# Placing the k-transpose-v tiles of a linear attention in other passes of its projection loop

## The chip, the cores and the metric

One NeuronCore of a Trainium2 chip runs the whole program as one launch. The metric is the device time of the launch in microseconds, taken as the median of several runs. PE stands for TensorE (its weight loads are shown as PEld), DVE for VectorE, ACT for ScalarE, POOL for GpSimd and SP for SyncE, whose queue issues nearly all DMAs.

## What is computed

The input x has 2048 rows of 640 elements, in bf16. The reference, cut to what matters:

```python
x = A_x
h  = x + A_ref(layernorm(x), wqkv, w_phi, wo)
h2 = h + (gelu(ln(h) @ w_gate) * (ln(h) @ w_up)) @ w_down

# A_ref: 32 heads of 20
q, k, v = split(x @ wqkv)
phi_q = concat(softmax(q @ w_phi), softmax(-(q @ w_phi)))     # per head, 40 features
phi_k = concat(softmax(k @ w_phi), softmax(-(k @ w_phi)))
kv = phi_k^T v          # per head, summed over all 2048 rows
z  = sum(phi_k)         # over all rows
o  = (phi_q kv) / (phi_q z + 1e-6)
return o @ wo
```

No row's attention output can be had before `kv` and `z` have been summed over all rows.

## The kernel before

Rows are worked in 16 tiles t of 128. `w_phi` is folded into the k and q weights on the chip (`fold`, L221), so `Wk2` and `Wq2` give the features' logits directly.

**The projection loop (L462 to L511) makes one pass per tile t.** `k_tile(t)` (L312) runs 10 matmuls into a PSUM tile `pk`, and ACT makes of it exp(x) and exp(-x), the tile `E` (two activations, L317). `v_mm(t+4)` runs 10 matmuls for the v of a later tile and `v_ev` (ACT, L304) copies it to `vS`. `ln_ap(t+6)` (ACT, L143) normalizes a later tile, and SP sends it through a transposing DMA into `LN1T` (L159), from which `v_mm` and `k_tile` read. `k_norm(t)` (L320) sums `E` per head on DVE (`sk`, L324), inverts the sums (`rs`, L328) and multiplies them into v, on POOL and DVE (`vt`, L332). `E` and `vt` have 8 buffers each.

**`kv_tile(i)` (L344) adds tile i to the sum.** It issues 40 small matmuls (128 rows by 32 columns of `E` against 42 or 63 columns of `vt`), each with its own weight load, thus 80 PE instructions, into one PSUM bank `kvp` that lives from pass 3 to the end of the loop. PE executes its instructions in the order in which the code issues them, so `KVG` (L56) says behind which pass's `k_tile` the sums of which tiles run: tiles 0 to 2 in pass 6, 3 to 5 in pass 9, 6 to 8 in pass 12, 9 to 11 in pass 15, and the last four after the loop (L513). Within a pass the order on PE is `k_tile(t)`, a fold of a part of `Wq2` (passes 10 to 14), the `kv_tile`s, then in pass 15 the q groups, then `v_mm(t+4)` (passes 1 to 11).

**The q groups.** `q_mm(j)` (L364) computes the q logits of group j of `QG` for 512 rows: two blocks of 5 matmuls of 512 columns for groups 0 to 2, one block for group 3. `q_exp(j)` (L376) lets ACT make the two exponentials `Eq`. `QT` (L53) puts groups 0 to 3 in pass 15. PSUM is shared by `pk`, `pv`, the fold and `pq` through 3 rotating tiles of two banks (`psG`, L465).

**After the loop** `kv_mask()` (L355, DVE) masks the sum into the matrix `KV`, the PSUM pools are closed and a pool of 4 tiles is opened (L520). PE goes on with the first block of q group 4 (L755), whose PSUM tile lies where group 3's was, with the first attention tile (`attn_a(0)`, matmuls at L562 on `KV` and `Eq`), and then with the remaining q groups, the attention tiles, and the feed-forward part (`gate_up` L685, `down` L702).

SP's queue in passes 7 to 13 carries, in this order, the transposes of the normalized tiles, those of the q weights (`load_T(WqT, ...)`, L194, in passes 7 to 10 by `LQ`), three small copies of `kmask` (L505), and the loads of `Wo` and `Wg` (L510, L511). The fold in pass 14 reads the last part of `WqT`.

Of the kernel before, what the change touches and what calls it, by code (L numbers as in the profile page):

```python
# [17 lines left out]
def kernel(  # L18
# [19 lines left out]
    NT = S // P  # L38
# [14 lines left out]
    QT = (15, 15, 15, 15)  # L53
    T3 = 3

    KVG = {6: (0, 1, 2), 9: (3, 4, 5), 12: (6, 7, 8), 15: (9, 10, 11)}  # L56
    VC = Dh + 1
    KC = Dh + 2

# [131 lines left out]
    def load_T(WT, i, *ds):  # L191

        for d in ds:
            nc.sync.dma_start_transpose(WT[:, :, d * P:(d + 1) * P], A_wqkv[d * P:(d + 1) * P, i * D:(i + 1) * D])  # L194
# [26 lines left out]
    def fold(WT, W2, quarters, ds=range(NC)):  # L221


        n, w = (2, QF) if quarters else (1, HD)
        runs = []
        for c in range(NC):
            lo, hi = H0[c] * Dh, (H0[c] + NH[c]) * Dh
            for r in range(2 * n):
                a, b = max(lo, r * w), min(hi, (r + 1) * w)
                if a < b:  # L230
                    runs.append((r // n, r, c, a, b))
        runs.sort()
        for d in ds:
            wa = gtile("wa")
            wr = wa.rearrange("p u (q x) -> p (u q) x", q=n)
            for i, (u, r, c, a, b) in enumerate(runs):
                nc.tensor.matmul(wr[:, r, a - r * w:b - r * w], lhsT=WT[:, c, d * P:(d + 1) * P],
                                 rhs=BD[:, c].rearrange("p a b -> p (a b)")[:, a - H0[c] * Dh:b - H0[c] * Dh],
                                 start=(i == 0 or runs[i - 1][0] != u),
                                 stop=(i + 1 == len(runs) or runs[i + 1][0] != u), skip_group_check=True)  # L240
            dst, src = W2[:, d, :].rearrange("p (u f) -> p u f", u=2), wr[:, :, 0:w]
            if quarters:
                dst = W2[:, d, :].rearrange("p (c r f) -> p r c f", c=NC, r=4)
                src = src.rearrange("p r (c f) -> p r c f", c=NC)
            if d in (QA if quarters else KA):
                nc.scalar.copy(dst, src)
            else:
                nc.vector.tensor_copy(dst, src)
# [15 lines left out]
    def ln_st(*tiles, act=True, between=None, log=False):  # L264
        for t, v in zip(tiles, ln_stats(p1, [x_sb[t // 4][:, t % 4, :] for t in tiles], "1", act, between, log)):
            lnp[t] = v

    def ln_ap(t, on_act=False, on_pe=False):
        ln = (ln_act if on_act else ln_dve)(p1, "1", *lnp[t])
        if on_pe:  # L270
            lnp[t] = ln
        else:
            transpose_to(LN1T[t // 4][:, :, t % 4 * P:(t % 4 + 1) * P], ln, False)
# [15 lines left out]
    def v_mm(t, us=(0, 1)):  # L289
        if 0 in us:  # L290
            pv[t] = gtile("pv")
        proj(pv[t], t, Wv, us)
# [10 lines left out]
    def v_ev(t):  # L303
        nc.scalar.activation(vS[t % 8][:, :, 0:Dh].rearrange("p (u h) f -> p u h f", u=2),  # L304
                             pv[t][:, :, 0:HD].rearrange("p u (h f) -> p u h f", f=Dh), ACTF.Copy,
                             scale=lnp[t][2] if t in CT else 1.0)
# [5 lines left out]
    def k_tile(t):  # L312
        pk = gtile("pk")
        proj(pk, t, Wk2, rows=t == 0)
        Ek[t] = ev.tile([P, 2, D], BF16, name="E", bufs=8)
        for s in range(2):
            nc.scalar.activation(Ek[t][:, s, :].rearrange("p (u f) -> p u f", u=2), pk[:, :, 0:HD],  # L317
                                 ACTF.Exp, scale=((lnp[t][2], nrstd[t]) if t in CT else (1.0, -1.0))[s])

    def k_norm(t):  # L320


        sk = small(p1, [P, 2 * H], "sk")
        nc.vector.reduce_sum(sk, Ek[t].rearrange("p s (h f) -> p (s h) f", f=Dh), axis=AX.X)  # L324
        if t - 1 in todo:
            todo.pop(t - 1)()
        rs = small(p1, [P, 2 * H], "rs")
        nc.vector.reciprocal(rs, sk)  # L328
        Vt[t] = vt = ev.tile([P, 2, H, VC], BF16, name="vt", bufs=8)

        def mult(s, eng):
            eng.tensor_tensor(vt[:, s], vS[t % 8], rs[:, s * H:(s + 1) * H, None].to_broadcast([P, H, VC]), ALU.mult)  # L332

        mult(1, nc.gpsimd)
        if t in VP:
            mult(0, nc.gpsimd)
        elif t == NT - 1:
            mult(0, nc.vector)
        else:
            todo[t] = lambda: mult(0, nc.vector)  # L340
# [3 lines left out]
    def kv_tile(t):  # L344

        for s in range(2):
            for c in range(NC):
                i, h, n = SLOT[c]
                for r in range(4):
                    f0, h0 = r * QF + c * 32, r * QH + h  # L350
                    nc.tensor.matmul(kvp[QUAD[r], s * SL + i:s * SL + i + n, :],
                                     lhsT=Ek[t][:, s, f0:f0 + 32], rhs=Vt[t][:, s, h0:h0 + n, :],
                                     start=(s == c == t == 0), stop=(t == NT - 1), skip_group_check=True)
# [10 lines left out]
    def q_mm(j, part=(0, 1)):  # L364

        if 0 in part:
            pqs[j] = gtile("pq")
        for i, bc in enumerate(QG[j]):
            if i not in part:
                continue  # L370
            b, c = divmod(bc, NC)
            for kc in range(NC):
                nc.tensor.matmul(pqs[j][:, i, :], lhsT=Wq2[:, kc, c * P:(c + 1) * P], rhs=LN1T[b][:, kc, :],  # L373
                                 start=(kc == 0), stop=(kc == NC - 1))

    def q_exp(j, signs=(0, 1)):  # L376
        for s in signs:
            nc.scalar.activation(Eq[j][:, :, s, :], pqs[j][:, 0:len(QG[j])], ACTF.Exp, scale=(1.0, -1.0)[s])  # L378
# [83 lines left out]
    for t in range(NT):  # L462
        if t == T3:
            ps_cm.close()
            psG = ps_cm.enter_context(tc.tile_pool(name="psG", bufs=3, space=PSUM, reuse_waits="tile"))  # L465
            psK = ps_cm.enter_context(tc.tile_pool(name="psK", bufs=1, space=PSUM, reuse_waits="tile"))
            kvp = psK.tile([P, 2 * SL, VC], F32, name="kvp")
        k_tile(t)
        if t == 0:
            ln_ap(6)  # L470
        if t in FQ:
            fold(WqT, Wq2, True, [i for i, f in enumerate(FQ) if f == t])
        for i in KVG.get(t, ()):
            kv_tile(i)
        for j in range(len(QT)):
            if t == QT[j]:
                q_mm(j)
                q_exp(j)
        if 0 < t < NT - 4:
            v_mm(t + 4)  # L480
        if t > 0 and t + 6 < NT:
            ln_ap(t + 6, on_act=True)
        if 0 < t < NT - 4:
            v_ev(t + 4)
        if t % 2 == 0 and t + 8 < NT:
            ln_st(t + 8, t + 9)
        k_norm(t)
        load_T(WqT, 0, *[i for i, f in enumerate(LQ) if f == t])
        if t == 10:
            transpose_to(LN1T[0][:, :, P:2 * P], ln_a(1), False)  # L490
        if t == 12:
            ln_ap(0, on_act=True)
        if t == 7:
            nc.gpsimd.memset(kmask[QUAD[0]], 1.0)
            for k, lo, n, base in ((3, 0, 2, 0), (2, 6, 3, 12)):
                m = kmask[QUAD[0], lo:lo + 6].rearrange("p (k n) -> p k n", k=k)
                nc.gpsimd.affine_select(out=m, in_=m, pattern=[[4, k], [-Dh, n]],
                                        compare_op=ALU.is_ge, fill=0.0, base=base, channel_multiplier=1)
                nc.gpsimd.affine_select(out=m, in_=m, pattern=[[-4, k], [Dh, n]],
                                        compare_op=ALU.is_ge, fill=0.0, base=Dh - 1 - base, channel_multiplier=-1)  # L500
        if t == 8:
            nc.gpsimd.memset(KV, 0.0)
        if t == 9:
            for r in (1, 2, 3):
                nc.sync.dma_start(kmask[QUAD[r]], kmask[QUAD[0]])  # L505
        if t == 11:
            nc.gpsimd.tensor_copy(KV[:, 0, :, KC - 1], kmask)
            nc.gpsimd.tensor_copy(KV[:, 1, :, 0], kmask)
        if t == 13:
            nc.sync.dma_start(Wo, wo_v)  # L510
            nc.sync.dma_start(Wg, wg_v)  # L511
    q = len(QT)
    for t in range(12, NT):  # L513
        kv_tile(t)
    kv_mask()
    ev_cm.__exit__(None, None, None)
# [341 lines left out]
```

## Time and profile before

| | |
|---|---|
| median of 3 runs | 279.61 us (279.37 to 279.69) |
| the profiled execution: its own time | 280.84 us |
| its span, first to last instruction | 278.9 us |
| PE busy / DVE / ACT / POOL | 97% / 62% / 51% / 34% of the span |
| PE matmuls, weight loads | 2979, 2995 |
| mean granted PE clock | 0.994 |
| instruction-fetch packets, queue q8 | 23, 0.38 MB |

The span leaves out 1.94 us of the execution's own time. In the timeline a row gives the start, the length, the engine, the line, the operation, its output and inputs, the count, and in brackets the idle time before it with what ended it. Matmul ends are modelled, so neighbouring rows of PE overlap a little; for PE the distance between two starts is the safer measure. A run of ten 320-column matmuls is followed by the next one 1.36 us later, a run of ten 512-column ones 2.16 us later.

### The profile page before, as it was taken

How to read it: one execution, taken by the hardware profiler on the slowest of the kernel's cores; microseconds unless marked ns; L12 is line 12 of the kernel's file. 1: busy time of each engine (PE TensorE's matmuls, PEld its weight loads, DVE VectorE, ACT ScalarE, POOL GpSimd, SP SyncE). 2: the span in 40 equal slices, each digit the busy share in tenths (PEclk: the TensorE clock that was granted, in tenths of full speed). 3: DMA queues.
4: the chain of work that ended last, by engine and by line, in shares of the span. 5: the costliest groups of instructions: out<-in, count | busy, mean ns of one | idle time of the engine just before them, and what ended most of it. 6: DMA issues, size and time to landing. Idle time of an engine off the chain costs nothing.

```text
span 278.9 us, 7232 instructions
## 1 busy us (share of the span) xinstructions
PE 270.4 (97%) x2979; PEld 172.5 (62%) x2995; DVE 173.6 (62%) x332; ACT 141.2 (51%) x241; POOL 95.8 (34%) x219
## 2 busy tenths in 40 slices
PE   8999899999699999999999999999999999999996
PEld 4777677764345688778864555575455567444574
DVE  4879999986368586676457874235986432233332
ACT  5789888887379866446533445402445420222200
POOL 4248999674001125645402372202155300000000
PEclk9999999999889999999999999999999999999999
DMA  6963616587049112224211222110213311000011
GB/s 185 205 232 67 72 34 113 54 181 290 5 129 382 58 27 44 53 51 95 49 49 47 27 47 58 38 48 26 49 27 71 46 47 49 24 0 0 2 47 47
DMA packets 42400, 21.46 MB, mean 77 GB/s; under 512 B 35200, under 2 KB 40576, under 8 KB 42368
## 3 DMA queue, kind: packets, MB, share of 16 engines
q1 hardware_dynamic: 41712, 20.98, 31.0%
q8 instruction: 23, 0.38, 0.6%
q10 hardware_dynamic: 656, 0.03, 0.2%
q14 instruction: 9, 0.07, 0.1%
HBM read 10.18 MB, written 2.62 MB: 46 GB/s over the span
## 4 chain that ended last, share of the span: by engine, by line
PE 72%; issue 1%; ACT 0%; DVE 0%
PE gu L694 37%; PE pd L713 19%; PE po L634 8%; PE pq L373 6%; PE ab L562 2%; PE tp L156 0%; ACT Eq L378 0%; DVE y L716 0%
## 5 line engine op out<-in xcount | busy, mean ns | idle before, releaser
L700 DVE TENSOR_TENSOR GT<-gu,g 128x512 bf16<-128x512 f32 (+1 forms) x60 | 34.4, 580 | 47.3 <-PE gu L694 38.5
L697 ACT ACTIVATE g<-gu 128x512 bf16<-128x512 f32 (+1 forms) x60 | 30.7, 512 | 63.7 <-PE gu L694 63.5
L694 PE MATMUL gu<-LN2T,Wg 128*128 128x512 bf16 (+1 forms) x289 | 61.2, 335 | 0.6
L694 PE MATMUL gu<-LN2T,Wu 128*128 128x512 bf16 (+1 forms) x300 | 61.7, 336 | 0.0
L713 PE MATMUL pd<-Wd,GT 128*128 128x320 bf16 (+2 forms) x396 | 53.5, 295 | 0.0
L713 PEld LDWEIGHTS <-GT 128*128 128x128 bf16 x396 | 37.9, 98 | 14.6 <-DVE GT L700 0.2
L694 PEld LDWEIGHTS <-Wu 128*128 128x128 bf16 x300 | 29.4, 98 | 22.6
L694 PEld LDWEIGHTS <-Wg 128*128 128x128 bf16 x300 | 28.6, 98 | 20.8
L284 PEld LDWEIGHTS <-LN1T 128*128 128x128 bf16 x290 | 27.7, 98 | 11.4 <-DMA LN1T<-ln 1.1
L716 DVE TENSOR_TENSOR y<-pd,x_sb 128x320 bf16<-128x320 f32 (+2 forms) x29 | 13.9, 480 | 29.4 <-PE pd L713 29.4
L332 POOL TENSOR_TENSOR vt<-vS,rs 128x672 bf16<-128x672 bf16 x22 | 29.2, 1346 | 7.6 <-DVE rs L328 3.4
L373 PE MATMUL pq<-LN1T,Wq 128*128 128x512 bf16 x95 | 24.3, 397 | 3.0 <-issue 2.8
L634 PE MATMUL po<-Wo,oT 128*128 128x320 bf16 x160 | 24.4, 299 | 0.0
L284 PE MATMUL pk<-Wk,LN1T 128*128 128x320 bf16 x160 | 24.2, 299 | 0.0
L324 DVE TENSOR_REDUCE sk<-E 128x64 f32<-128x1280 bf16 x16 | 22.9, 1433 | 0.6 <-ACT E L317 0.6
L378 ACT ACTIVATE Eq<-pq 128x1024 bf16<-128x1024 f32 (+1 forms) x26 | 20.0, 829 | 4.5 <-PE pq L373 4.5
L284 PE MATMUL pv<-Wv,LN1T 128*128 128x320 bf16 x130 | 19.8, 299 | 0.7 <-DMA LN1T<-ln 0.7
L317 ACT ACTIVATE E<-pk 128x640 bf16<-128x640 f32 x28 | 18.2, 706 | 3.5 <-PE pk L284 3.4
L634 PEld LDWEIGHTS <-oT 128*128 128x128 bf16 x160 | 15.5, 98 | 7.0 <-ACT oT L157 0.5
L611 DVE TENSOR_TENSOR tt<-AB,w 128x1280 bf16<-128x1280 f32 x12 | 17.8, 1486 | 1.0 <-POOL w L604 0.9
L143 ACT ACTIVATE ln<-x_sb,v,rstd 128x640 bf16<-128x640 bf16 x14 | 12.9, 921 | 10.7 <-POOL v L673 10.3
L373 PEld LDWEIGHTS <-Wq 128*128 128x128 bf16 x100 | 9.7, 102 | 13.7 <-issue 4.8
(114 smaller groups left out, 288.4 us busy)
## 6 DMA issues: line engine op xcount, KB each, us to landing
out_dram<-y SPq DMA_DIRECT2D x15, 160.0 KB, 1.9
Wg<-in_B_w_gate_dram SPq DMA_DIRECT2D x1, 1920.0 KB, 10.3
Wu<-in_B_w_up_dram SPq DMA_DIRECT2D x1, 1920.0 KB, 8.8
Wd<-in_B_w_down_dram SPq DMA_DIRECT2D x2, 960.0 KB, 11.0
x_sb<-in_A_x_dram SPq DMA_DIRECT2D x2, 640.0 KB, 6.2
Wo<-in_A_wo_dram SPq DMA_DIRECT2D x1, 800.0 KB, 5.0
x_sb<-in_A_x_dram SPq DMA_DIRECT2D x4, 160.0 KB, 4.5
Wv<-in_A_wqkv_dram SPq DMA_DIRECT2D x2, 320.0 KB, 5.0
```

Source lines behind the costliest of these rows:

```text
L284: nc.tensor.matmul(ps[:, u, 0:HD], lhsT=lnT(t, c), rhs=W[:, c, u * HD:(u + 1) * HD], start=(c == 0), stop=(c == NC - 1))
L317: nc.scalar.activation(Ek[t][:, s, :].rearrange("p (u f) -> p u f", u=2), pk[:, :, 0:HD], ACTF.Exp, scale=((lnp[t][2], nrstd[t]) if t in C ...
L324: nc.vector.reduce_sum(sk, Ek[t].rearrange("p s (h f) -> p (s h) f", f=Dh), axis=AX.X)
L332: eng.tensor_tensor(vt[:, s], vS[t % 8], rs[:, s * H:(s + 1) * H, None].to_broadcast([P, H, VC]), ALU.mult)
L373: nc.tensor.matmul(pqs[j][:, i, :], lhsT=Wq2[:, kc, c * P:(c + 1) * P], rhs=LN1T[b][:, kc, :], start=(kc == 0), stop=(kc == NC - 1))
L378: nc.scalar.activation(Eq[j][:, :, s, :], pqs[j][:, 0:len(QG[j])], ACTF.Exp, scale=(1.0, -1.0)[s])
L611: nc.vector.tensor_tensor(tt.rearrange("p s (h f) -> p s h f", f=Dh), num, w[:, :, :, None].to_broadcast([P, 2, H, Dh]), ALU.mult)
L634: nc.tensor.matmul(pos[u], lhsT=st[t][:, c, :], rhs=Wo[:, c, u * HD:(u + 1) * HD], start=(c == 0), stop=(c == NC - 1))
L694: nc.tensor.matmul(gu[i][:, 0:n], lhsT=W[:, c, f * P:(f + 1) * P], rhs=LN2T[b][:, c, a0:a1], start=(c == 0), stop=(c == NC - 1))
L697: nc.scalar.activation(g[:, 0:n], gu[0][:, 0:n], ACTF.Gelu_apprx_tanh)
L700: nc.vector.tensor_tensor(st[b, "g", f][:, a0:a1], gu[1][:, 0:n], g[:, 0:n], ALU.mult)
L713: nc.tensor.matmul(ps, lhsT=st[b, "g", f][:, tl * P:(tl + 1) * P], rhs=Wd[:, f, f0:f1], start=(f == 0), stop=(f == NF - 1))
```

## The change

The sums of tiles 0 to 9 run in groups of two, four and four, in passes 5, 9 and 13; those of tiles 10 to 12 run in pass 15 between q group 0 and q group 1; those of tiles 13 to 15 run after the loop, behind q group 3. Each `kv_tile` is the same as before, and they run in the same order.

```diff
-    KVG = {6: (0, 1, 2), 9: (3, 4, 5), 12: (6, 7, 8), 15: (9, 10, 11)}
+    KVG = {5: (0, 1), 9: (2, 3, 4, 5), 13: (6, 7, 8, 9)}
+    KVQ = {0: (10, 11, 12)}
...
             if t == QT[j]:
                 q_mm(j)
                 q_exp(j)
+                for i in KVQ.get(j, ()):
+                    kv_tile(i)
         if 0 < t < NT - 4:
             v_mm(t + 4)
...
     q = len(QT)
-    for t in range(12, NT):
+    for t in range(13, NT):
         kv_tile(t)
     kv_mask()
```

## Prediction

> **What bounds the kernel now.** I read the page first. The chain that ended last is PE's, for as far back as it could be followed:
>
> ```profile
> PE 72%; issue 1%; ACT 0%; DVE 0%
> ```
>
> PE is 97% busy, so work on other engines counts only where PE waits for it, and a mere reordering of PE's work gains only what PE loses in waits. The chain in order of time begins at the only large one (start, length, what):
>
> ```profile
> 70.69 0.50 ACT Eq L378
> 71.19 2.06 issue
> 73.25 0.39 PE pq L373
> ```
>
> ACT's last exponential of q group 3 frees the PSUM tile that the first block of group 4 needs, and then PE still starts 2.06 us later, with nothing that the profile shows in between. The timeline shows the same place and two smaller ones:
>
> ```profile
> 29.18 1.52 PE L284 MATMUL pk<-Wk,LN1T 128*128 128x320 bf16 x10
> 31.44 1.53 PE L284 MATMUL pv<-Wv,LN1T 128*128 128x320 bf16 x10 [0.74 <-DMA LN1T<-ln]
> ...
> 58.70 0.36 PEld L237 LDWEIGHTS <-WqT 128*128 128x128 bf16 x8 [0.41 <-DMA WqT<-in_A_wqkv_dram]
> ...
> 60.50 1.14 PE L351 MATMUL kvp<-vt,E 128*32 128x42 bf16 x120
> 61.58 7.73 PE L373 MATMUL pq<-LN1T,Wq 128*128 128x512 bf16 x34
> 69.23 1.47 PE L351 MATMUL kvp<-vt,E 128*32 128x42 bf16 x160
> 73.25 1.25 PE L373 MATMUL pq<-LN1T,Wq 128*128 128x512 bf16 x4 [2.55 <-issue]
> ```
>
> The reader is to see: 2.55 us of idle PE behind the last four tiles; 0.74 us in pass 5, where the v of tile 9 waits for a transpose; 0.41 us in pass 14, where the last fold waits for `WqT`. One kv tile costs 1.47/4 = 0.37 us. The table of stretches tells what follows the large hole (PE, PEld, DVE, ACT, POOL, then clock):
>
> ```profile
> 70.80:73.20 2.40, 0.00 (x0) 0.00 (x0) 0.86 (x2) 0.38 (x1) 0.00 (x0) 1.00 0.02 7
> 74.70:78.10 3.40, 3.18 (x35) 1.29 (x21) 2.77 (x7) 1.63 (x2) 0.00 (x0) 0.51 0.00 0
> 30.40:33.80 3.40, 2.66 (x21) 1.72 (x19) 3.30 (x9) 3.14 (x5) 3.31 (x4) 1.00 0.30 57
> ```
>
> The clock granted to PE falls to 0.51 for 3.4 us, which costs 0.49 x 3.4 = 1.7 us of a PE that is the bound; the hole of 0.74 us costs no clock. So the hole at 70.7 is worth 2.55 + 1.7 = 4.25 us.
>
> **Why 2.06 us of nothing.** I take it for PE's instruction supply. Queue q8 moves 0.38 MB in 23 packets for 2979 + 2995 PE instructions: one packet per 260. One lies inside the hole, the next shortly after it:
>
> ```profile
> q8 instruction: 1, 0.02, 11.7%
> ```
>
> This is the DMA view of 70.5 to 71 (the same view has one between 74 and 74.5, none between). The next was asked for, I think, when PE went on at 73.25, so asking to packet is 0.8 to 1.2 us. The packet in the hole was then asked for at about 69.5, and 73.25 - 69.5 = 3.7 us is asking to use. The four tiles are 320 instructions in 1.47 us: more than one packet's worth, faster than a packet comes. Shorter bursts of 240 at 34.26, 43.63, 54.16 and 60.50 end without a hole.
>
> **The change part by part.**
>
> *Tiles 0 and 1 in pass 5.* Tile 1's `vt` is complete at 29.1 (DVE row L332, 28.27 + 0.85). PE is free from 29.18 + 1.36 = 30.54 to 31.44, 0.90 us; two tiles take 0.73. They cost nothing, and the group in pass 6 (60.50 to 61.58 shows its price, 1.1) is gone: -0.73 us at the end of the group in pass 9. If the cover fails, +0.73 there.
>
> *Four tiles in pass 9 and in pass 13.* PE is 1.2 us ahead in passes 6 to 9. Who is late next? The transposes of tiles 10 and 11 land at 32.8 and 36.1 (issue plus 2.6 or 3.3) for starts at 34.2 and 36.9; ACT, with 1.30 + 0.92 + 0.71 = 2.93 us per pass against PE's 2.72, is still ready, since it had gaps of 0.4 to 0.65 before its rows. Landings of up to 4.2 us occur in the DMA view; one would cost up to 0.9. `vt` of tile 5 is done at 41.8, of tile 9 at 52.9, both ahead of their groups at about 42.4 and 55. `E` and `vt` buffers of tiles 10 and 14 wait for sums that stand earlier on PE: nothing.
>
> *Pass 14.* The fold waits for `WqT`, landed at 58.66 and issued at the end of a solid row of SP issues that begins with ACT's tile 14 at 43.16. If ACT's tile 14 moves 1.0 us forward with PE, so do these issues, and `Wo` and `Wg` behind them; otherwise PE waits here and loses its lead. The end of k tile 15 is thus S = 59.5 to 60.45 (before 60.41). Likeliest 59.5.
>
> *Pass 15.* Group 0 now starts at S, S + 2.16 it ends, three tiles take 1.10, groups 1 to 3 end at S + 5.42, 7.58, 8.66, the last three tiles at S + 9.76. The `Wq2` cast (ACT, ends 60.65 before) is needed only by the fifth matmul, at S + 0.9; `vt` of tile 12 is done at 60.7, tile 15 at 68.6. ACT: group 2's exponentials run from S + 7.78 to S + 9.72, group 3's to S + 10.7. The data let group 4 start at S + 10.75 = 70.25 (71.2 with the late S), before at 71.25.
>
> *The last burst.* It is 240 instructions, not 320. Count PE's instructions back from its end, as both kernels have the same ones behind it. 260 back lies 60 into the old burst, 1.2 us before its end. In the new order it lies 20 ahead of the burst, 3.3 us before the end; with what PE's queue holds in advance (some 45, from the packets' places in the gate stretch) it lies inside tiles 10 to 12, 6.6 us before. Needed are 3.7: supply is ready between 0.4 us after the tiles' end and well before it, and the data come 1.0 after it. Against this: while `Wg` streams at some 400 GB/s, the packet at 64.7 came 347 instructions after its predecessor, about 3.8 us after being due. That much delay puts the start at up to 72. I take 70.6, nearer the data end: 73.25 - 70.6 = -2.65 us (bounds -3.0 and -1.2).
>
> *The clock.* The new hole is 70.6 less 69.3 = 1.3 us (1.0 to 2.0), between the row of 0.74 that cost nothing and 2.55 that cost 1.7 us; nearer the first, so I take the loss as gone, bounds 0 and -1.7. With PE faster there, attention tile 1 needs group 4's exponentials (1.94 us) about when they end; I keep -1.45.
>
> Sum: -2.65 - 1.45 = -4.1 us on the profiled 280.84 gives 276.7. The median of the runs, 1.23 us below that execution, gives 279.61 - 4.1 = **275.5**.
>
> [...]
>
> **Rivals.**
>
> *The hole shrinks and the clock stays as it is*, because 1.3 to 2 us still bring it down, or because the unprofiled runs never had the loss (they are 1.23 us shorter): -2.65, 277.0; range 276.4 to 278.
>
> *The 2.06 us are a fixed price* of the new PSUM pool or of a wait that isn't shown. Then group 4 starts at 70.2 + 2.06 = 72.3, the clock still falls: -0.95, 278.65. For it: the hole stands exactly at the pool's change. Against it: the packet inside it.
>
> *Nothing is gained*: the late `WqT` and the late packet eat it, 279.3 to 280.1.
>
> *Slower: groups of four starve PE wherever they stand.* Place: passes 9 and 13. Price: 2.06 us each, less the 0.73 of pass 5, and a clock loss of 1.7 each in place of the one at the end; the tail gains its 2.0. 4.1 + 3.4 - 1.7 - 0.7 - 2.0 = +3.1, 282.7. It decides when a packet is asked for in the first 60 of the 320 instructions, as in the last group now. My count backwards puts the askings about 110 to 170 into them, with 150 to 210 left of the group and slow k matmuls behind: against it.
>
> **How the numbers follow.** Forecast 0.52 (274.4 to 276.4), clock unchanged 0.18, fixed price 0.14, nothing 0.08, slower 0.08. The range 274.4 to 278.7 takes in the first three, 0.84 of the chance. Two tenths of a per cent, 0.56 us, is about what can be told from no change: faster 0.84, same 0.08, slower 0.08.
>
> **What would show it.** Two kvp tiles in the hole at 30.5, the v of tile 9 still at 31.4; k tile 15 ending near 59.5; no PE hole behind the groups of four; a packet of q8 between 66 and 69.5 and the first block of group 4 within 0.3 us of ACT's last exponential of group 3; clock 1.0 from 70 to 80. Wrong, if 2 us of "issue" remain before group 4, if the fold of pass 14 waits over 1 us, or if a hole opens in group 2.

## The result, and the profile after

| | before | changed |
|---|---|---|
| median of 6 runs, first comparison | 279.49 us (278.59 to 279.69) | 276.57 us (276.11 to 277.47) |
| ratio, 95% interval | | 0.9905 [0.9884, 0.9925] |
| profiled execution: time, span | 280.84, 278.9 us | 276.65, 274.7 us |
| mean granted PE clock of the profiled execution | 0.994 | 0.999 |

The change made the kernel faster, by 0.95% with an interval of 0.75 to 1.16%: 2.9 us between the medians, 4.2 us between the two profiled executions. The forecast was 275.5 us in a range from 274.4 to 278.7; the measured median lies in that range, but not in the narrower one of 274.4 to 276.4 that the forecast had for itself without its rivals.

The chain of work that ended last, of the changed kernel, at the place where 2.06 us of "issue" stood (start, length, what):

```profile
70.10 0.50 ACT Eq L379
70.60 0.04 issue
70.64 0.38 PE pq L374
```

Group 4 starts 0.04 us after ACT's last exponential of group 3. The timeline of PE, in the same three places as before:

```profile
28.78 1.52 PE L285 MATMUL pk<-Wk,LN1T 128*128 128x320 bf16 x10
30.23 0.94 PE L352 MATMUL kvp<-vt,E 128*32 128x42 bf16 x80
31.25 1.53 PE L285 MATMUL pv<-Wv,LN1T 128*128 128x320 bf16 x10
...
47.40 1.53 PE L285 MATMUL pv<-Wv,LN1T 128*128 128x320 bf16 x10 [0.31 <-DMA LN1T<-ln]
...
55.30 1.52 PE L352 MATMUL kvp<-vt,E 128*32 128x42 bf16 x160
56.76 1.53 PE L285 MATMUL pk<-Wk,LN1T 128*128 128x320 bf16 x10
58.13 0.50 PE L238 MATMUL wa<-BD,WqT 128*128 128x140 bf16 x8
58.46 1.52 PE L285 MATMUL pk<-Wk,LN1T 128*128 128x320 bf16 x10
59.82 2.32 PE L374 MATMUL pq<-LN1T,Wq 128*128 128x512 bf16 x9
62.07 1.14 PE L352 MATMUL kvp<-vt,E 128*32 128x42 bf16 x120
...
68.64 1.14 PE L352 MATMUL kvp<-vt,E 128*32 128x42 bf16 x120
70.64 1.24 PE L374 MATMUL pq<-LN1T,Wq 128*128 128x512 bf16 x4 [0.86 <-ACT Eq L379]
```

The wait of pass 5 holds two tiles now, the group of four at 55.30 is followed at once by the next k tile, the fold of pass 14 (58.13) no longer waits for `WqT`, and a new wait of 0.31 us stands at 47.40. The table of stretches (PE, PEld, DVE, ACT, POOL, then clock) shows no fall of the clock behind the smaller hole:

```profile
67.90:71.30 3.40, 2.49 (x127) 1.63 (x127) 0.88 (x2) 2.69 (x4) 0.48 (x1) 1.00 0.00 2
71.30:74.70 3.40, 3.35 (x54) 1.64 (x54) 2.03 (x6) 1.95 (x3) 0.00 (x0) 1.00 0.02 5
74.70:78.10 3.40, 3.35 (x54) 1.55 (x53) 2.50 (x5) 2.75 (x4) 0.77 (x1) 1.00 0.24 26
```

**Where the 4.25 us between the two spans come from.** Take three marks in each trace: the start of k tile 5 (29.18 and 28.78), the start of group 4 (73.25 and 70.64), the end (278.91 and 274.66). The change touches nothing ahead of the first mark, and 0.40 us were gained there: the start of the kernel varies from execution to execution. Between the first and the second mark 44.07 became 41.86: -2.21 us. Behind the second, 205.66 became 204.02: -1.64 us, the half-clock stretch. Two traces further down (`p5` and `b_shift256`) have the hole and the full clock, and they show that this last part is the clock alone: from the start of group 4 to the start of the last DVE operation it is 203.05 us in the kernel before, 201.41 in the changed one, and 201.43 and 201.42 in those two.

### The profile page after: what moved, and what is told of

The parts are those of the page before. It is cut to its first block, busy times and chain, and to the rows that moved or that the text cites. A ratio compares the mean times of both kernels' runs of the same rounds, so it can differ in the third digit from the quotient of the medians.

```text
span 274.7 us, 7230 instructions
## 1 busy us (share of the span) xinstructions
PE 268.2 (98%) x2978; PEld 171.7 (63%) x2995; DVE 174.2 (63%) x332; ACT 141.1 (51%) x241; POOL 96.6 (35%) x219
## 4 chain that ended last, share of the span: by engine, by line
PE 73%; issue 0%; ACT 0%; DVE 0%
PE gu L697 38%; PE pd L716 19%; PE po L637 8%; PE pq L374 5%; PE ab L565 2%; PE tp L157 0%; ACT Eq L379 0%; DVE y L719 0%
## 5 line engine op out<-in xcount | busy, mean ns | idle before, releaser
L374 PE MATMUL pq<-LN1T,Wq 128*128 128x512 bf16 x94 | 22.9, 379 | 1.2 <-ACT Eq L379 0.9
```

## The experiments

All runs are compared with runs of the kernel before on the same chip. The kernel before has two kinds of executions: in 24 of 65 the mean granted clock is 0.993 or 0.994 (median 279.9 us), in 41 it is 0.999 or 1.0 (278.4 us). One stretch of 3.41 us at half clock takes 0.006 off the mean of 279 us, so the first kind is what one such stretch makes; only one execution of it was traced. Where a median of "full-clock" runs is named, it is that of the second kind. One more, at 0.988 (282.17 us), is counted in neither.

### Moving the packet boundaries, and nothing else

The theory says that PE's instructions come in packets of a fixed count (23 packets for 5974 instructions make 260; the expectations reckon with 256, a count that the second of these runs tests), and that the hole stands where a packet ends and the next hasn't come. If so, a few instructions more or fewer at the very start must move the hole. Four kernels with the old order differ from the kernel before in the warm-up matmuls alone, whose results nobody reads; the columns in all stay the same but for a few.

42 instructions more (`b_shift42`):

```diff
-    warm(*[512] * 7, *[P] * 8)
+    for n in [128] * 36:
+        nc.tensor.matmul(wu[0:32, 0, 0:n], lhsT=ones[:, 0:32], rhs=ones[:, 0:n], start=True, stop=True)
```

> The old order; only the 15 warm-up matmuls at the start are cut into 36 short ones of the same 4608 columns in all, which puts 42 more PE instructions ahead of everything at no more PE time. Supply theory (a packet of 256 PE instructions is asked for when PE's queue crosses a fixed multiple of 256, and is of use 3.7 us later): the packet that was asked for at the start of the last burst of 320 (69.4 us) is now asked for 42 instructions earlier, in q groups 2 and 3, about 2.5 us sooner. So group 4 starts when ACT's last exponential ends (71.3 instead of 73.25), the 2.06 us of issue are gone, the clock doesn't fall: -1.9 and -1.7 us, -3 to -3.6 in all. Rival (the 2.06 us belong to the change of the PSUM pool, or to any burst of four tiles): nothing changes, the hole stays at 2.5 us, the time within 0.5 us of the kernel before.

Measured: 277.86 us, ratio 0.9947 [0.9925, 0.997]; all 12 runs at full clock. The chain at group 4:

```profile
71.15 0.50 ACT Eq L379
71.65 0.04 issue
71.69 1.24 PE pq L374 x5
```

The hole is gone without any change to the order of the work. The total gain is smaller than expected: 1.6 us between the medians, 0.5 us against full-clock runs. In part that is the start: another packet now comes at 26.85, while the transpose of tile 8 is under way, and pass 4 waits 1.25 us for that transpose, where pass 5 had waited 0.74. The rest of the shortfall, some 0.9 us of the 1.9 that were expected from the hole alone, isn't explained; the traced execution of the kernel before, from which the 1.9 were read, was itself longer than most.

256 more, one whole packet by the theory, as a control (`b_shift256`; `for n in [32] * 143`):

> The control of b_shift42: the old order, the warm-up cut into 143 matmuls of 32 columns, 256 more PE instructions ahead of everything, exactly one packet. Supply theory: every packet boundary stands where it stood against the work, so the hole of 2.5 us before group 4 and the fall of the clock stay, and the time is within 0.7 us of the kernel before. If the cut warm-up itself (and not where the boundaries lie) were what helped in b_shift42, this one would be faster too, by about 3 us.

Measured: 281.3 us, ratio 1.0071 [1.0043, 1.0098]; clock low in 5 of 12 runs. The chain:

```profile
72.34 0.50 ACT Eq L379
72.84 1.99 issue
74.83 1.25 PE pq L374 x5
```

The hole is back, again right ahead of group 4's first matmul, so a shift of 256 instructions leaves it where it was; and so is the fall of the clock in part of the runs. That the time is 2 us over the kernel before was not expected. In its trace two places of the start are worse: the first v matmuls start at 7.69 instead of 7.06, behind the DMA of `Wv`, and the k tile at 26.03 starts 1.66 us late, which the profile puts down to ACT's copy `vS`. I didn't follow up their causes.

22 more (`b_shift22`; `for n in [177] * 26`):

> The old order with half the shift of b_shift42: the warm-up cut into 26 matmuls of about the same columns in all, 22 more PE instructions. Supply theory: the packet is asked for 22 instructions before the point where it was asked for in the old order, that is just ahead of the last burst, some 0.3 to 0.8 us sooner, against 2.5 us in b_shift42. So about half of the 2 us of issue ahead of group 4 is left: 1.2 to 1.7 us. Rival (a prologue with more and shorter warm-up matmuls takes the hole away by itself, or all or nothing): 0 or 2 us.

Measured: 277.84 us, ratio 0.9962 [0.9939, 0.9984]. PE's timeline:

```profile
69.58 1.38 PE L352 MATMUL kvp<-vt,E 128*32 128x42 bf16 x149
71.94 0.26 PE L352 MATMUL kvp<-vt,E 128*32 128x42 bf16 x11 [0.98 <-issue]
72.13 1.25 PE L374 MATMUL pq<-LN1T,Wq 128*128 128x512 bf16 x4
```

I had expected a shorter wait ahead of group 4. The wait is shorter (0.98), but it is in the middle of the last burst, after 149 of its 160 matmuls. That is 298 of 320 instructions: the hole moved forward by exactly the 22 that were added. My expectation had the right theory and forgot that the place moves with it. The time is 0.5 us under full-clock runs.

12 fewer (`b_9`):

```diff
-    warm(*[512] * 7, *[P] * 8)
+    warm(*[512] * 9)
```

> The old order with a shift the other way: the same 4608 warm-up columns as 9 matmuls instead of 15, 12 PE instructions fewer ahead of everything. Supply theory: the boundary moves 12 instructions past the last kv matmul, so the 10 instructions of group 4's first block are already there. Group 4 starts with ACT's last exponential, 0.05 us of issue, and the wait moves behind that block: the first attention tile (ab) starts 0.4 to 0.9 us after the block's end, and nothing ends that wait but issue. The time falls by about 1.2 us against full-clock runs of the kernel before. Rival (the wait belongs to the change of the PSUM pool, or more instructions ahead are what helps): the hole of 2 us stays ahead of group 4.

Measured: 277.43 us, ratio 0.9954 [0.9932, 0.9975]. PE's timeline:

```profile
71.04 1.24 PE L373 MATMUL pq<-LN1T,Wq 128*128 128x512 bf16 x4 [0.52 <-ACT Eq L378]
72.21 0.19 PE L562 MATMUL ab<-KV,Eq 32*128 32x44 bf16 x1
72.57 0.46 PE L562 MATMUL ab<-KV,Eq 32*128 32x44 bf16 x39 [0.17 <-issue]
```

Group 4 starts with ACT, runs its 10 instructions, the first attention matmul and its weight load run, and then PE stands: 12 instructions behind the old place, as many as were taken out. Start to start it is 0.36 us, a little less than expected, and so is the gain, 0.9 us against full-clock runs where 1.2 were expected. The four together show what the 2.06 us are: PE stands at a fixed count of its own instructions, wherever that count falls. A price of the PSUM pool's change is excluded.

The DMA records of the traces show a packet each time. In the kernel before, the packet of q8 in the hole runs from 70.83 to 71.76, and PE goes on at 73.25, 1.49 us after its end. In the traces of `b_shift256`, `b_shift22` and `b_9`, and in those of `p5` and `each` below, a packet ends 1.49, 1.43, 1.37, 1.47 and 1.41 us before PE goes on.

### The change in parts

Groups of two and four in passes 5 and 9 alone (`p5`):

```diff
-    KVG = {6: (0, 1, 2), 9: (3, 4, 5), 12: (6, 7, 8), 15: (9, 10, 11)}
+    KVG = {5: (0, 1), 9: (2, 3, 4, 5), 12: (6, 7, 8), 15: (9, 10, 11)}
```

> One part alone: groups of two and four in passes 5 and 9, the rest of the old order (three tiles in pass 12, three in pass 15 ahead of q group 0, four at the end). All packet boundaries stand at the old places of the last burst. My theory: tiles 0 and 1 fill the wait for the transpose in pass 5, PE keeps a lead of 0.7 to 1.0 us up to q group 0, and the hole before group 4 (2.5 us) and the fall of the clock stay: -0.7 to -1.0 us. Rival (the lead is lost again at a later transpose or at the WqT wait of pass 14): within 0.3 us of the kernel before.

Measured: 278.87 us, ratio 0.9978 [0.9951, 1.0005], so by itself it isn't clear of no change; at full clock 277.9 in 6 runs (-0.5 us), at low clock 279.6 in 6. The hole stays, 2.63 us of idle PE, and the execution traced here has the full clock all the same:

```profile
69.21 0.50 ACT Eq L378
69.70 2.15 issue
71.85 1.25 PE pq L373 x5
```

Only three tiles after the loop:

```diff
-    KVG = {6: (0, 1, 2), 9: (3, 4, 5), 12: (6, 7, 8), 15: (9, 10, 11)}
+    KVG = {6: (0, 1, 2), 9: (3, 4, 5), 12: (6, 7, 8), 15: (9, 10, 11, 12)}
...
-    for t in range(12, NT):
+    for t in range(13, NT):
```

> The other part alone: passes 6, 9 and 12 as before, four tiles in pass 15 ahead of q group 0, three after the loop. Supply theory: the packet for group 4 is asked for long before the last burst, so group 4 starts at 71.5 to 72.0 (ACT's exponentials end 0.36 us later than before, at 71.5), and the clock doesn't fall: -1.3 to -1.7 and -1.7 us, about -3.1 in all, that is most of the change's gain. Rival (the gain comes from the q group that starts early, tiles 10 to 12 behind it): -0.4 us at most, hole of 2 us and more.

Measured: 277.2 us, ratio 0.9923 [0.9893, 0.9953], all runs at full clock; -1.2 us against full-clock runs, and 0.04 us of issue ahead of group 4. The gain was expected at 3.1, of which 1.7 were charged to a clock loss that only a part of the old executions have; of the rest, 1.3 to 1.7, nearly all came.

Tiles 10 to 12 behind q group 0 and three after the loop, the passes before as in the old order (`KVG` as before with `15: (9,)`, `KVQ = {0: (10, 11, 12)}`):

> The last third of the change alone: passes 6, 9 and 12 as before, one tile in pass 15 ahead of q group 0, tiles 10 to 12 behind it, three after the loop. Supply theory: it is worth what the run with only a shorter last burst (four tiles ahead of group 0, three at the end) was, since 13 tiles stand ahead of groups 1 to 3 in both: no issue ahead of group 4, clock full, -1.0 to -1.4 us against full-clock runs of the kernel before, within 0.3 us of that run. Rival (the early start of group 0 is worth something by itself, as ACT starts its exponentials 1 us sooner): 0.5 to 1 us better than that run.

Measured: 277.3 us, ratio 0.9948 [0.9928, 0.9969]; 0.04 us of issue; 0.1 us from the run before. So the early start of group 0 is worth nothing that can be told, and the two halves add up: -0.5 for pass 5, -1.1 to -1.2 for the shorter last burst, against -1.7 for the whole change (276.65 over 13 runs against 278.4), all at full clock.

### Is the changed kernel still short of instructions?

One tile behind each of groups 0 to 2 (`each`):

```diff
-    KVQ = {0: (10, 11, 12)}
+    KVQ = {0: (10,), 1: (11,), 2: (12,)}
```

> The changed kernel, but tiles 10, 11 and 12 go one behind each of q groups 0, 1 and 2 instead of all behind group 0. ACT gets group 2's logits at the same time, group 1's 0.7 us sooner. By the order of PE's work alone nothing changes for group 2 (three tiles stand ahead of it in either order), except that tile 12 now stands behind it: group 2 ends 0.37 us sooner and with it ACT's last exponential, -0.35 us. By the supply theory the packet for group 4 is now asked for inside tile 12, about 1 us ahead of the last burst, and is of use about 0.5 us after ACT is done: issue of 0.3 to 0.7 us ahead of group 4, and no gain against the changed kernel (0 +- 0.3 us).

Measured: 276.72 us, ratio 0.9917 [0.9885, 0.9948], no gain against the changed kernel, as expected. The chain of the traced execution, the longest of the six (277.90), has the issue that was expected, slightly more of it:

```profile
70.84 0.50 ACT Eq L379
71.34 0.80 issue
72.14 0.39 PE pq L374
```

The same with the 9-matmul warm-up:

> The same as the run with one tile behind each of q groups 0 to 2, with the warm-up as 9 matmuls (12 PE instructions fewer). Supply theory: the boundary moves past group 4's first block, whose 1.08 us now cover the rest of the packet's way: no issue ahead of group 4, none ahead of ab, and the 0.35 us of ACT's earlier end are kept: -0.3 to -0.5 us against the changed kernel. Rival (PE is not short of instructions there): both runs are equal to each other.

Measured: 276.0 us, ratio 0.9893 [0.9862, 0.9923]. No issue is left:

```profile
69.56 0.50 ACT Eq L379
70.06 0.04 issue
70.10 0.38 PE pq L374
```

The order of the work is the same in both, and twelve instructions fewer at the start go with 0.7 us less, though the intervals overlap. Against the changed kernel it is -0.6 us, a little more than expected. In a last comparison on one chip:

> The changed kernel once more, as the yardstick on the same chip for the other runs of this call. 2.5 to 3 us under the median of the kernel before, 1.6 to 2.0 us under its full-clock runs.

> The changed kernel with the warm-up as 9 matmuls (12 PE instructions fewer), its tiles where the change puts them. Supply theory: group 4 of the changed kernel is bound by ACT's last exponential and not by instructions, so nothing is gained: 0 +- 0.3 us against the changed kernel. Rival (the 9 matmuls of the warm-up are better by themselves): 0.5 us faster, as in the run with one tile behind each group.

> One tile behind each of q groups 0 to 2 and the warm-up as 9 matmuls, once more, beside the changed kernel on the same chip. ACT's last exponential ends about 0.35 us sooner relative to the start of group 0 and no instructions are missing: -0.3 to -0.5 us against the changed kernel. If the two differ by less than 0.2 us, the earlier 0.5 us were a difference between chips.

Measured: the changed kernel 276.86 us, ratio 0.993 [0.9906, 0.9955]; with the 9-matmul warm-up 276.35, 0.9911 [0.9892, 0.993]; one tile behind each group with that warm-up 275.99, 0.9898 [0.9878, 0.9918]. The first is 1.6 us under the full-clock runs of the kernel before, as expected, but only 1.7 under the median of all, where 2.5 to 3 were expected: here 2 of 12 runs had the low clock. The last is 0.9 us under the changed kernel, where 0.3 to 0.5 were expected. The second expectation missed: the changed kernel with 9 warm-up matmuls is 0.5 us faster, the figure of the rival, though the intervals overlap. The traced execution of the changed kernel, the longest of its seven (277.82), shows what the other warm-up can spare it:

```profile
71.06 0.50 ACT Eq L379
71.56 0.22 issue
71.78 0.39 PE pq L374
```

and in its timeline

```profile
47.94 0.85 PE L285 MATMUL pv<-Wv,LN1T 128*128 128x320 bf16 x5 [0.71 <-DMA LN1T<-ln]
```

The changed kernel is at the edge: in this execution 0.22 us of issue came back, and the transpose of tile 14 was late by 0.71 us (0.31 in the first one). The trace with 9 warm-up matmuls shows neither. Whether the 9 matmuls help only by way of the packets' places isn't shown. With that warm-up in both, one tile behind each group is worth another 0.36 us, the 0.35 by which ACT's last exponential was to end sooner. The kernel with one tile behind each group and 9 warm-up matmuls took 275.7 to 276.4 us in 12 runs on two chips; 10 of the 13 runs of the changed kernel are longer than all of these. It is the best version seen, by some 0.7 us in the medians, though the intervals of the ratios overlap.

## Why the prediction was right, and where it was off

**The hole as instruction supply: right, shown.** The four shifted kernels put the stop at 298, 320 and 332 instructions from the start of the last burst, and out of sight, just as instructions were added or removed. When a packet is asked for was only reckoned (3.7 us before its use); what the traces show is the 1.4 to 1.5 us from a packet's end to PE going on. The control, with the hole in its old place after 256 more instructions, bears out a packet of 256. How far ahead of its use PE's supply comes isn't shown by any run; the 45 instructions in the prediction were an estimate from the packets' places.

**Two tiles in pass 5: right in kind, and the lead was mis-sized.** The two tiles run from 30.23, in the old wait. The lead should have brought k tile 15's end to 59.5; it came at 59.82, of which 0.40 us are the earlier start of that execution. Counted from k tile 5, only 0.2 us were won there, with one tile more already done (0.37), where 0.9 were predicted. Half a microsecond went where the prediction had seen a danger ("Landings of up to 4.2 us occur in the DMA view; one would cost up to 0.9"): the transpose of tile 14 landed late and took 0.48 us between matmuls at 46.9. Another 0.2 went in pass 5 itself: from k tile 5 to k tile 6 it is 3.84 us, before 3.63, so the two tiles did not cost quite nothing. In `p5`, the run with the groups of passes 5 and 9 alone, the lead was kept and was worth 0.5 us.

**The rival that groups of four in passes 9 and 13 starve PE: wrong, as argued.** The one at 55.30 is followed directly; the one in pass 9 took 1.6 us instead of 1.5.

**Start of group 4: 70.64, predicted 70.6**, but from k tile 5 on it is -2.21 us instead of -2.65; the agreement is in part the 0.40 us of the start, that is, luck. It starts 0.04 us after ACT's last exponential, within the 0.3 us that were predicted. The hole ahead of it is 0.86 us and not 1.3, since the last burst ended later than reckoned. The fear that `Wg`'s stream delays the packet wasn't tested: a packet of q8 lies at 64 to 64.5 in the changed kernel, where the DMAs move 426 GB/s, and the next at 67.5 to 68, between the predicted 66 and 69.5. In the second trace of the changed kernel the two lie at 65.45 and 69.31, the later one ends at 70.19, and group 4 starts 1.59 us after that with 0.22 us of issue. That is the edge on which the changed kernel stands.

**The clock: the right mechanism, charged too often.** With the hole the half-clock stretch costs 1.64 us between the two traces, predicted 1.45. But it was charged to every execution of the kernel before, on the strength of one trace and of three times that lay together. It strikes 24 of 65. The two other kernels with such a hole (2.63 us of idle PE in the trace of `p5`, 2.47 in that of `b_shift256`) show a low mean clock in part of their runs (6 of 12, 5 of 12); those whose traces have no hole over 1.25 us in 0 of 83. So the size of the hole doesn't decide it alone: of the three traces with it, only that of the kernel before shows the fall.

What may decide is when the hole falls. In the trace of the kernel before, the record of the clock begins with full at 6.47, goes to half at 74.74 and back to full at 78.15, for 201.39 us: 20 steps of 3.41 us, then one, then 59. In the changed kernel's trace the first full stretch, from 4.54 on, is 269.65 us, 79 such steps. Counted in such steps from where each trace's own record begins, the hole puts 1.92 us of idle PE into the step just ahead of the fall; in `p5` it is split into 1.86 and 0.77, in `b_shift256` into 1.06 and 1.41. PE was still busy for 1.43 us in the step ahead of the fall. Three traces can't give a limit, and that the idle time of one step decides is a guess which no run tests.

**The sum.** -4.1 us were predicted on the profiled execution, and 4.19 came (4.25 on the span), but from other terms: 2.21 for the hole where 2.65 stood, 1.64 for the clock where 1.45 stood, and 0.40 from the start of the kernel, which the change doesn't touch. That the sum fits so well is luck. On the medians it was 2.9 of 4.1, in the later comparisons 1.7 (full-clock runs). The failing step is the last one, that the difference of one traced execution may be set on the median: that execution had the low clock and was also 0.95 us longer than the median of its own kind (279.9). How those 0.95 us divide between its start and a longer hole stays open, since there is one trace of the kernel before. Of the rivals, "the hole shrinks and the clock stays as it is" (277.0, range 276.4 to 278) came nearer to the median of 276.57 than the forecast did, 0.4 us against 1.1. Its second reason, that other executions never had the loss, holds for 41 of the 65 runs; its -2.65 us for the hole is too much as well. The 2.9 us of the first comparison lie between the two readings: the clock of its six runs of the kernel before isn't on record, but four of them took 279.4 to 279.7 us, as low-clock runs do.

## What to carry to other kernels

A hole on PE that nothing in the profile ends, right behind a long burst of small instructions (here 2.06 us of issue behind 320 of them, 160 matmuls with their weight loads in 1.47 us), should be checked against the instruction queue's packets: add or drop a few instructions far ahead and see whether the hole moves by that count. The remedy that worked here was a last burst of 240 instructions with slow q matmuls ahead of it (0.04 us of issue in `tail3` and in the changed kernel's first trace, 0.22 in its second). A long burst isn't harmful everywhere: the groups of 320 in passes 9 and 13 took 0.2 us more at most in the changed kernel's first trace. Before a saving from one traced execution is set on a median, look at the granted clock of many runs: a loss that strikes some of them (here 24 of 65) is worth only its share.

## What the runs showed that I had not expected

In these traces a packet that falls on a transposing DMA under way goes with a longer landing. In those of the kernel before and of the changed one the median transpose into `LN1T` lands 2.6 us after its issue; the eight in whose time a packet began took 3.2 to 4.6 us, the others 2.6 to 3.1. In the kernel before, with a packet at 28.5, that of tile 9 takes 4.0 us and that of tile 8 takes 2.6; in `b_shift42`, with the packet at 26.85, that of tile 8 takes 4.4 and that of tile 9 takes 2.6. In the changed kernel it is 4.6 for that of tile 14, with a packet at 44.8. What joins the two isn't shown. With 42 more instructions at the start the wait thus moved from pass 5 (0.74 us) to pass 4 (1.25), and with 12 fewer it grew to 1.20 in pass 5.

The start varies too: k tile 5 begins at 28.78 and at 29.23 in the two traces of the changed kernel, the same code.
